# Attention decode over a cached GQA block: values as the streamed operand in four column groups, with the wanted tiles picked out by masks

## The chip, the cores and the metric

The kernel runs on one core of a Trainium2 chip. The metric is device time in microseconds (us) of one execution; the time of a version is the median of several executions. One more execution was recorded by the hardware profiler, and all lines of profile here come from it. PE is the matrix engine (TensorE), DVE the vector engine (VectorE), ACT the scalar engine (ScalarE), POOL GpSimd, and SP the engine that issues the DMAs.

## What is computed

Two layers, each an attention block with a cache and then a gated feed-forward block, with the same weights and the same cache in both. One new token for each of 4 sequences; 32 query heads share 8 key/value heads; 8192 cached positions of 128 numbers. Everything is bf16 at the inputs.

```python
def _A_ref(x, k_cache, v_cache, wq, wo):          # x: 4 x 1 x 512
    q = (x @ wq).reshape(B, Sq, 32, 128).transpose(0, 2, 1, 3)
    k = jnp.repeat(k_cache, 4, axis=1)            # cache: 4 x 8 x 8192 x 128
    v = jnp.repeat(v_cache, 4, axis=1)
    scores = jnp.einsum("bhqd,bhkd->bhqk", q, k) * (128 ** -0.5)
    p = softmax(scores, axis=-1)
    o = jnp.einsum("bhqk,bhkd->bhqd", p, v)
    return o.transpose(0, 2, 1, 3).reshape(B, Sq, 32 * 128) @ wo

def _B_ref(x, w_gate, w_up, w_down):
    return (silu(x @ w_gate) * (x @ w_up)) @ w_down

x = A_x
x = x + _A_ref(layernorm(x), ...)
x = x + _B_ref(layernorm(x), ...)
x = x + _A_ref(layernorm(x), ...)
x = x + _B_ref(layernorm(x), ...)
```

## The kernel before

**Units.** A unit is one key/value head `g` of one sequence `b`: 32 units a layer, 2 MB of keys and 2 MB of values each. SBUF has 8 slots of 2 MB (`kvf`); each load is one DMA from SP (`pump`, L307), issued as soon as a slot is free. Partition p of a slot holds positions 64p to 64p+63, so a slot is 64 tiles of 128 columns (one tile: one position from each partition). Three units of layer 0 stay in slots and are the first of layer 1. The feed-forward weights use two of the slots at the end of each layer; there the last seven loads are kept out of these two slots, and the very last V comes in four quarters (`split`, `NQ`).

**Keys.** DVE turns each eighth of a K slot in 32x32 blocks (`turn`, L392, eight 128x512 operations a unit). PE multiplies it with the queries (`scores`, L412, 4 matmuls of 256 columns an eighth). The scores of a unit are one 128x256 tile of PSUM: row 32a + 4q + h, column 32t' + i hold head h, and tile t = 8q + t' (q is the eighth, t' the tile within it).

**Softmax**, as five steps (`max_p`, `max_t`, `exps`, `turn_p`, `total`): row maximum on DVE (L418), turned on PE (L422), maximum per head on DVE (L425), spread by ACT (L428) and PE (L434), ACT for the bias (L437), the exponentials (L438) and their sums per head (L440), 32x32 transposes of the probabilities on DVE (L443), the total on PE (L446) and its reciprocal on DVE (L448).

**Values** (`values`, L482). For each tile t the 128x128 value tile is the stationary operand, and 32 columns of the turned probabilities stream past it, of which the first four are wanted; 64 matmuls accumulate into columns 0 to 31 of a PSUM bank (L493). The result is oT: output dimension on partitions, heads on columns. One DVE operation scales the four wanted columns (`scale_o`, L501). After the fourth unit of a head group `out_proj` multiplies with `wo` (L522, L525, L528, L513).

**What sets the order.** Each engine runs its instructions in the order in which the program issues them. Key and value work is a list of `blocks` with a cost in us each; `drain` runs them and after each lets `advance` take that cost off the first entry of `line`, the list of the small steps. A step is issued when its own gap has run down. `flush(u)` issues everything in `line` up to the steps of unit u before its values. When a unit's values are through, `scale_o` (and `out_proj` if it is due) go to the front of `line`. `turn` is issued when `keys` is called, about 2 us of blocks ahead of the scores. `_Sync` (L24 to L95) adds the semaphore waits.

**The ends of a layer.** After the last values come `out_proj`, `center`, the gate and up products (`ffn`, L599), the down products (L616), and in the last layer the transposes of the output (L665). The next layer's first key load goes into the slot that the gate and up weights used.

Of the kernel before, what the change touches and what calls it, by code (L numbers as in the profile page):

```python
# [103 lines left out]
def bass_interleave_layers__gqa_block_cached__swiglu_ffn__decode_kernel(  # L104
# [17 lines left out]
    REP = Hq // G  # L122
# [15 lines left out]
    NQ = 4  # L138
    NSLOT = 8
    NKEEP = 6  # L140
    WIDE = 32
# [4 lines left out]
    with ExitStack() as es:  # L146
# [32 lines left out]
        xx = sb("xx", [P, XB], FP32)  # L179
        lnv = sb("lnv", [P, B], FP32)  # L180
        rstd = sb("rstd", [P, B], FP32)
        xc = sb("xc", [P, XB], FP32)
        xn = sb("xn", [P, XB], BF16)
        oT = sb("oT", [P, Hq, B], BF16)
# [6 lines left out]
        pT = sb("pT", [P, 2, SW + WIDE], BF16)  # L191
        qT = pT[:, 1, 0:XQ].rearrange("p (b h) -> p b h", b=B)
        rl = sb("rl", [P, 2, REP], FP32)
        xoT = sb("xoT", [P, XB], BF16)
# [41 lines left out]
        for a in range(NA):  # L236
# [6 lines left out]
        T.op("dve", lambda e: e.memset(pT[:, :, SW:], 0.0), writes=["pT0", "pT1"])  # L243
        T.op("dve", lambda e: e.tensor_reduce(head[:], identf[:].rearrange("p (x h) -> p h x", h=REP), AX.X, ALU.max),
             reads=["ident"], writes=["head"])
        nc.scalar.preload_act_table_set("natural_log_exp_and_others")
# [195 lines left out]
        def turn_p(u):  # L442
            T.op("dve", lambda e: e.transpose(pT[:, turn_of[u], 0:SW], pb[:]), reads=["pb"], writes=[f"pT{turn_of[u]}"])  # L443
# [38 lines left out]
        def values(L, u):  # L482
            g, b = unit_gb(u)
            bk = OBK[turn_of[u]]

            def block(q):
                if q == 0:
                    flush(u)
                s = slot_of["V", L, u]

                for t in range(q * TB, (q + 1) * TB):
                    c0 = (t % TB) * QB + REP * q
                    T.op("pe", lambda e: e.matmul(bank(bk)[:, 0:WIDE], lhsT=kv[:, s, t * Dh:(t + 1) * Dh],  # L493
                                                  rhs=pT[:, turn_of[u], c0:c0 + WIDE], start=(t == 0), stop=(t == TT - 1)),
                         reads=[f"s{s}.{q}", f"pT{turn_of[u]}"], writes=[f"pb{bk}"], sig=(t % TB == TB - 1))
                if q == NB - 1:
                    finished(("V", L, u))
                    line[0:0] = rest

            def scale_o():  # L500
                T.op("dve", lambda e: e.tensor_tensor(oT[:, g * REP:(g + 1) * REP, b], bank(bk)[:, 0:REP],  # L501
                                                      rl[:, turn_of[u], :], ALU.mult),
                     reads=[f"pb{bk}", f"rl{turn_of[u]}"], writes=["oT"])

            rest = [[0.3, None, scale_o]]
            done.add((L, u))
            if all((L, g * B + k) in done for k in range(B)):
                rest.append([0.5, None, lambda: out_proj(g)])
            blocks.extend((0.2, lambda q=q: block(q)) for q in range(NB))
# [6 lines left out]
        def out_proj(g):  # L516

            pick = ident.rearrange("p (j e) -> p e j", e=REP)
            ob = bank(OUTB)[:, XB:2 * XB].rearrange("p (e b) -> p e b", b=B)
            for c in range(REP):  # L520
                for h in range(REP):
                    T.op("pe", lambda e: e.matmul(ob[h * QB:(h + 1) * QB, c, :], lhsT=pick[:, c, :],  # L522
                                                  rhs=oT[:, g * REP + h, :], start=True, stop=True),
                         reads=["oT", "ident"], writes=[f"pb{OUTB}"], sig=(h == REP - 1))
            T.op("dve", lambda e: e.tensor_copy(o4[:], ob), reads=[f"pb{OUTB}"], writes=["o4"])  # L525
            for nt in range(KT):
                for c in range(REP):
                    T.op("pe", lambda e: e.matmul(bank(OUTB)[:, nt * B:(nt + 1) * B],  # L528
                                                  lhsT=wo_sb[:, g, c, nt * P:(nt + 1) * P], rhs=o4[:, c, :],
                                                  start=(c == 0), stop=(c == REP - 1)),  # L530
                         reads=[f"wo{g // (G // 4)}", "o4"], writes=[f"pb{OUTB}"], sig=(c == REP - 1))
            add_to_x()
# [5 lines left out]
        def center():  # L538
# [8 lines left out]
            T.op("dve", lambda e: e.scalar_tensor_tensor(bk3(xc[:]), total, -1.0 / D, bk3(xT[:]),  # L547
                                                         op0=ALU.mult, op1=ALU.add),
                 reads=["x", f"pb{LNB}"], writes=["xc"])
            T.op("dve", lambda e: e.tensor_tensor(xx[:], xc[:], xc[:], ALU.mult), reads=["xc"], writes=["xx"])  # L550
            T.op("dve", lambda e: e.tensor_reduce(vs[:], xx[:].rearrange("p (k b) -> p b k", b=B), AX.X, ALU.add),
                 reads=["xx"], writes=["vs"])
# [34 lines left out]
        def ffn(last):  # L587
# [37 lines left out]
            if last:  # L625
                T.op("dve", lambda e: e.tensor_tensor(xoT[:], xT[:], bank(dn[-1])[:, 0:XB], ALU.add),
                     reads=["x", f"pb{dn[-1]}"], writes=["xoT"])
            else:
                add_to_x(dn[-1])
# [34 lines left out]
        for kt in range(KT):  # L664
            T.op("pe", lambda e: e.matmul(ob[0:B, kt * P:(kt + 1) * P], lhsT=xoT[:, kt * B:(kt + 1) * B],  # L665
                                          rhs=ident, is_transpose=True, start=True, stop=True),
                 reads=["xoT", "ident"], writes=[f"pb{LNB}"], sig=(kt == KT - 1))
# [32 lines left out]
```

## Time and profile before

| | |
|---|---|
| median of 3 runs | 665.35 us (664.87 to 666.32) |
| the profiled execution, its own time | 666.57 us |
| its span, first to last instruction | 664.7 us |
| PE, DVE, ACT busy | 502.1, 382.1, 89.9 us |
| HBM read | 273.88 MB, 412 GB/s over the span |
| mean granted PE clock | 0.82 |

A line of a group reads: line of the kernel, engine, operation, output<-input, shape, count | busy us in total, mean ns of one | idle us of the engine just before them, and what ended most of it. A line of the timeline reads: start us, duration us, engine, line, operation, count, and in brackets the idle time before it and what ended it. The DMA row gives the mean busy share of the 16 DMA engines in each of 40 slices, in tenths.

The chain that ended last, followed back from the last instruction, is made up of these shares of the span:

```profile
DMA 70%; PE 20%; DVE 4%; SPq 3%; issue 2%; POOL 0%; ACT 0%; DVEq 0%; POOLq 0%
```

### The profile page before, as it was taken

The page shows a single profiled execution, that of the slowest core. Times are in us where ns is not written, and L with a number is a line of the kernel's source. Part 1 is how long each engine was busy: PE and PEld are TensorE (multiplying, and loading weights), DVE is VectorE, ACT ScalarE, POOL GpSimd, SP SyncE. Part 2 cuts the span into 40 slices and gives each one's busy share as a digit, 9 for nine tenths or more (in the row PEclk, how much of TensorE's full clock was granted, in tenths as well). Part 3 has the DMA queues.
Part 4 walks back from the last instruction along what each step waited for, and adds up shares of the span by engine and source line. Part 5 has one row for each costly group of instructions (what it writes and reads, how often), then busy time and mean ns, then how long its engine had stood idle before and what let it go on. Part 6 is the DMA issues. An engine that isn't in the chain of part 4 may idle for free.

```text
span 664.7 us, 17302 instructions
## 1 busy us (share of the span) xinstructions
PE 502.1 (76%) x7656; PEld 400.1 (60%) x7656; DVE 382.1 (57%) x895; ACT 89.9 (14%) x331; POOL 19.9 (3%) x75
## 2 busy tenths in 40 slices
PE   1767687777768787876876999887787696786796
PEld 1545565655646565664664878765566565575575
DVE  1646475565566465575731289766566566566572
ACT  1010110110101110110110112110111110110120
POOL 0000000000000000000000000000000000000000
PEclk9887789877878778797785979986878977788885
DMA  9999999999999999999998899999999999999995
GB/s 366 424 423 418 430 431 423 425 425 429 427 424 425 427 426 425 426 428 424 424 404 344 331 426 430 425 424 427 426 427 424 428 426 426 426 425 429 425 414 210
DMA packets 23963, 275.00 MB, mean 414 GB/s; under 512 B 2376, under 2 KB 2384, under 8 KB 7888
## 3 DMA queue, kind: packets, MB, share of 16 engines
q1 hardware_dynamic: 23888, 273.89, 98.0%
q8 instruction: 60, 0.98, 0.6%
q14 instruction: 15, 0.12, 0.0%
HBM read 273.88 MB, written 0.00 MB: 412 GB/s over the span
## 4 chain that ended last, share of the span: by engine, by line
DMA 70%; PE 20%; DVE 4%; SPq 3%; issue 2%; POOL 0%; ACT 0%; DVEq 0%; POOLq 0%
DMA kvf<-in_A_k_cache_dram 68%; PE ps L412 13%; SPq L93 3%; DMA kvf<-in_B_w_down_dram 2%; DVE kvf L392 2%; PE ps L493 2%; PE ps L434 1%; PE ps L422 1%; DVE one L418 1%; PE ps L599 0%; PE ps L566 0%; PE ps L616 0%; DVE rl L448 0%; PE ps L446 0%; PE ps L541 0%
## 5 line engine op out<-in xcount | busy, mean ns | idle before, releaser
L392 DVE STREAM_TRANSPOSE kvf<-kvf 128x512 f32<-128x512 f32 x488 | 313.1, 677 | 193.5 <-DMA kvf<-in_A_k_cache_dram 193.5
L412 PE MATMUL ps<-kvf,zq 128*128 128x256 bf16 x2048 | 331.2, 318 | 9.5 <-DVE kvf L392 7.1
L412 PEld LDWEIGHTS ps<-kvf,zq 128*128 128x128 bf16 x2048 | 215.1, 113 | 69.4 <-DVE kvf L392 9.8
L493 PE MATMUL ps<-pT,kvf 128*128 128x32 bf16 x4096 | 123.0, 178 | 16.3 <-DVE rl L448 15.1
L493 PEld LDWEIGHTS ps<-pT,kvf 128*128 128x128 bf16 x4096 | 120.0, 97 | 23.9 <-issue 19.4
L422 PE MATMUL ps<-identf,one 128*1 128x128 f32 x64 | 19.2, 301 | 103.7 <-DVE one L418 103.7
L428 ACT ACTIVATE pb<-m 1x128 f32<-1x128 f32 x64 | 19.7, 308 | 391.9 <-DVE m L425 391.9
L422 PEld LDWEIGHTS ps<-identf,one 128*1 128x1 f32 x64 | 5.2, 81 | 107.7 <-DVE one L418 107.5
L403 POOL TENSOR_TENSOR zq<-scr,quad 128x64 bf16<-128x64 bf16 x64 | 18.8, 293 | 617.9 <-PE ps L412 550.5
L434 PEld LDWEIGHTS ps<-one,pb 1*128 1x128 f32 x128 | 24.4, 237 | 20.3 <-issue 18.1
L418 DVE TENSOR_REDUCE one<-ps 128x1 f32<-128x256 f32 x64 | 25.2, 394 | 10.6 <-PE ps L412 10.6
L443 DVE STREAM_TRANSPOSE pT<-pb 128x256 bf16<-128x256 bf16 x64 | 26.4, 412 | 8.3 <-ACT pb L438 7.7
L438 ACT ACTIVATE pb<-ps,one 128x256 bf16<-128x256 f32 x64 | 30.4, 474 | 2.1
L434 PE MATMUL ps<-one,pb 1*128 1x1 f32 x128 | 29.9, 300 | 0.5 <-ACT pb L428 0.5
L437 ACT ACTIVATE one<-ps 128x1 f32<-128x1 f32 x64 | 11.0, 171 | 137.2 <-PE ps L434 137.2
L446 PEld LDWEIGHTS ps<-rsm,one 128*128 128x128 f32 x128 | 20.8, 204 | 2.8 <-ACT rsm L440 0.6
L446 PE MATMUL ps<-rsm,one 128*128 128x4 f32 x128 | 19.8, 225 | 0.5 <-ACT rsm L440 0.5
L440 ACT ACTIVATE rsm<-head,one 128x4 f32<-128x4 f32 x64 | 19.0, 297 | 2.1
L425 DVE TENSOR_REDUCE m<-ps 1x4 f32<-1x128 f32 x64 | 15.9, 248 | 5.7 <-PE ps L422 5.0
L501 DVE TENSOR_TENSOR oT<-ps,rl 128x4 bf16<-128x4 f32 x64 | 7.9, 123 | 9.3 <-PE ps L493 8.9
L528 PE MATMUL ps<-o,wo_sb 128*128 128x4 bf16 x256 | 9.2, 167 | 4.9 <-DVE o L525 4.9
L513 DVE TENSOR_TENSOR xT<-xT,ps 128x16 f32<-128x16 f32 x21 | 3.6, 172 | 15.2 <-PE ps L528 11.1
(57 smaller groups left out, 108.3 us busy)
## 6 DMA issues: line engine op xcount, KB each, us to landing
kvf<-in_A_k_cache_dram SPq DMA_DIRECT2D x61, 2048.0 KB, 31.7
kvf<-in_A_v_cache_dram SPq DMA_DIRECT2D x58, 2048.0 KB, 32.3
wq_sb<-in_A_wq_dram SPq DMA_DIRECT2D x4, 1024.0 KB, 7.6
wo_sb<-in_A_wo_dram SPq DMA_DIRECT2D x4, 1024.0 KB, 35.2
kvf<-in_A_v_cache_dram SPq DMA_DIRECT2D x8, 512.0 KB, 19.7
kvf<-in_B_w_gate_dram SPq DMA_DIRECT2D x2, 1792.0 KB, 24.1
kvf<-in_B_w_down_dram SPq DMA_DIRECT2D x4, 768.0 KB, 16.3
kvf<-in_A_v_cache_dram SPq DMA_DIRECT2D x2, 1024.0 KB, 5.0
```

The source lines that it names most:

```text
L93: ins = self.eng[engname].dma_start(out_ap, in_ap)
L392: T.op("dve", lambda e: e.transpose(w, w), reads=[f"s{s}.{q}"], writes=[f"s{s}.{q}"])
L412: T.op("pe", lambda e: e.matmul(bank(bk)[:, 0:SW], lhsT=zq[:, c, z0:z0 + P], rhs=w[:, :, c // 2, :, c % 2], start=(q == 0 and c == 0), sto ...
L418: T.op("dve", lambda e: e.tensor_reduce(mx[:], bank(bk)[:, 0:SW], AX.X, ALU.max), reads=[f"pb{bk}"], writes=["mx"])
L422: T.op("pe", lambda e: e.matmul(bank(STEP)[0:1, 0:P], lhsT=mx[:], rhs=identf[:], is_transpose=True, start=True, stop=True), reads=["mx", " ...
L428: T.op("act", lambda e: e.activation(mrow.rearrange("p (x h) -> p x h", h=REP), m4[:].unsqueeze(1).to_broadcast([1, QB, REP]), ACTF.Copy), ...
L434: T.op("pe", lambda e: e.matmul(bank(STEP)[:, 0:1], lhsT=mrow, rhs=onesf[0:1, :], start=True, stop=True), reads=["pb", "onesf"], writes=[f ...
L438: T.op("act", lambda e: e.activation(pb[:], bank(bk)[:, 0:SW], ACTF.Exp, bias=nm[:], accum_out=rs[:]), reads=[f"pb{bk}", "nm"], writes=["p ...
L440: T.op("act", lambda e: e.activation(rsm[:], head[:], ACTF.Copy, scale=rs[:]), reads=["head", "rs"], writes=["rsm"])
L443: T.op("dve", lambda e: e.transpose(pT[:, turn_of[u], 0:SW], pb[:]), reads=["pb"], writes=[f"pT{turn_of[u]}"])
L446: T.op("pe", lambda e: e.matmul(bank(TOT)[:, 0:REP], lhsT=ones, rhs=rsm[:], start=True, stop=True), reads=["rsm", "onesf"], writes=[f"pb{T ...
L493: T.op("pe", lambda e: e.matmul(bank(bk)[:, 0:WIDE], lhsT=kv[:, s, t * Dh:(t + 1) * Dh], rhs=pT[:, turn_of[u], c0:c0 + WIDE], start=(t == ...
```

## The change

The operands of the value product swap places. Now 16 columns of the turned probabilities are the stationary operand and four value tiles (512 columns) stream past them. `NQ` becomes 2, `NV` = 4. A unit has two halves i; a half has 8 matmuls, one for each tile number t within the eighths; each streams tile t of the eighths 4i to 4i+3, and its 16 weight columns are those of the same four eighths, four heads each. Matmul t writes to the 16 partitions from 32 (t mod 4), so four column groups of the array are used in turn. A row of the result (eighth y, head h) holds four blocks of 128 columns, of which only block y is the row's own; the others are products with the wrong tile.

`own_tile` takes each row's own block: ACT copies block 0 scaled by mask column 0 into `acc` (128x128 fp32), and three DVE operations add blocks 1, 2, 3 times their masks (`own`, built at the start). `scale_o` then multiplies `acc` as weights with `head` (fp32, 4 columns) on PE, which adds the rows of one head over column groups and eighths and turns the result, and DVE scales it. `acc` is one buffer, shared by all units and, in its first columns, by `xc` and `xx` of `center`.

The last V of each layer comes in two halves. The two output banks are zeroed at the start, as the unwritten partitions of them are read. `oT` keeps two groups, and `xoT` is gone (`xn` serves). In `line`, the steps after a unit's values go behind earlier such steps but ahead of softmax steps that wait.

```diff
-    NQ = 4
+    NQ = 2
...
-    WIDE = 32
+    NV = NB // NQ
+    assert TB == 2 * NA and NV * REP <= QB
...
+        acc = sb("acc", [P, Dh], FP32)
+        own = sb("own", [P, NV], FP32)
+        xc, xx = acc[:, 0:XB], acc[:, XB:2 * XB]
...
+        T.op("dve", lambda e: e.memset(ps[:, OBK[0] * BANKF:(OBK[1] + 1) * BANKF], 0.0), writes=[f"pb{k}" for k in OBK])
...
+        T.op("dve", lambda e: e.tensor_reduce(acc[:, 0:QB], identf[:].rearrange("p (y h) -> p y h", h=REP), AX.X, ALU.max),
+             reads=["ident"], writes=["acc"])
+        T.op("dve", lambda e: e.tensor_reduce(own[:], acc[:, 0:QB].rearrange("p (a y) -> p y a", a=NA)[:, 0:NV, :],
+                                              AX.X, ALU.max),
+             reads=["acc"], writes=["own"])
...
-            def block(q):
-                if q == 0:
+            def block(i):
+
+                if i == 0:
                     flush(u)
                 s = slot_of["V", L, u]
-
-                for t in range(q * TB, (q + 1) * TB):
-                    c0 = (t % TB) * QB + REP * q
-                    T.op("pe", lambda e: e.matmul(bank(bk)[:, 0:WIDE], lhsT=kv[:, s, t * Dh:(t + 1) * Dh],
-                                                  rhs=pT[:, turn_of[u], c0:c0 + WIDE], start=(t == 0), stop=(t == TT - 1)),
-                         reads=[f"s{s}.{q}", f"pT{turn_of[u]}"], writes=[f"pb{bk}"], sig=(t % TB == TB - 1))
-                if q == NB - 1:
+                v = kv[:, s, :].rearrange("p (q t d) -> p t q d", t=TB, d=Dh)
+                for t in range(TB):
+                    j = t % NA
+                    c0 = t * QB + i * NV * REP
+                    T.op("pe", lambda e: e.matmul(bank(bk)[j * QB:j * QB + NV * REP, :],
+                                                  lhsT=pT[:, turn_of[u], c0:c0 + NV * REP], rhs=v[:, t, NV * i:NV * (i + 1), :],
+                                                  start=(i == 0 and t == j), stop=(i == NQ - 1 and t >= TB - NA)),
+                         reads=[f"s{s}.{NV * i + k}" for k in range(NV)] + [f"pT{turn_of[u]}"], writes=[f"pb{bk}"],
+                         sig=(t == TB - 1))
+                if i == NQ - 1:
                     finished(("V", L, u))
-                    line[0:0] = rest
+                    n = len([1 for x in line if x[1] is None])
+                    line[n:n] = rest
+
+            def own_tile():
+                T.op("act", lambda e: e.activation(acc[:], bank(bk)[:, 0:Dh], ACTF.Copy, scale=own[:, 0:1]),
+                     reads=[f"pb{bk}", "own"], writes=["acc"])
+                for k in range(1, NV):
+                    T.op("dve", lambda e: e.scalar_tensor_tensor(acc[:], bank(bk)[:, k * Dh:(k + 1) * Dh], own[:, k:k + 1],
+                                                                 acc[:], op0=ALU.mult, op1=ALU.add),
+                         reads=[f"pb{bk}", "own", "acc"], writes=["acc"])
 
             def scale_o():
-                T.op("dve", lambda e: e.tensor_tensor(oT[:, g * REP:(g + 1) * REP, b], bank(bk)[:, 0:REP],
-                                                      rl[:, turn_of[u], :], ALU.mult),
-                     reads=[f"pb{bk}", f"rl{turn_of[u]}"], writes=["oT"])
-
-            rest = [[0.3, None, scale_o]]
+                T.op("pe", lambda e: e.matmul(bank(LNB)[:, 0:REP], lhsT=acc[:], rhs=head[:], start=True, stop=True),
+                     reads=["acc", "head"], writes=[f"pb{LNB}"])
+                T.op("dve", lambda e: e.tensor_tensor(oT[:, g // (G - 1), :, b], bank(LNB)[:, 0:REP], rl[:, turn_of[u], :],
+                                                      ALU.mult),
+                     reads=[f"pb{LNB}", f"rl{turn_of[u]}"], writes=[f"oT{g // (G - 1)}"])
+
+            rest = [[0.1, None, own_tile], [1.0, None, scale_o]]
...
-            blocks.extend((0.2, lambda q=q: block(q)) for q in range(NB))
+            blocks.extend((0.8, lambda i=i: block(i)) for i in range(NQ))
```

## The prediction

> **What bounds the kernel now.** I read the page from the top (DMA rows, queues, chain), then windows of the layer ends, then the timeline there. First the page:
>
> ```profile
> DMA  9999999999999999999998899999999999999995
> q1 hardware_dynamic: 23888, 273.89, 98.0%
> q8 instruction: 60, 0.98, 0.6%
> L392 DVE STREAM_TRANSPOSE kvf<-kvf 128x512 f32<-128x512 f32 x488 | 313.1, 677 | 193.5 <-DMA kvf<-in_A_k_cache_dram 193.5
> L493 PE MATMUL ps<-pT,kvf 128*128 128x32 bf16 x4096 | 123.0, 178 | 16.3 <-DVE rl L448 15.1
> kvf<-in_A_v_cache_dram SPq DMA_DIRECT2D x58, 2048.0 KB, 32.3
> ```
>
> The reader is to see that the 16 DMA engines are full nearly throughout, that VectorE waits 193.5 us for keys, and that a load lands some 32 us after its issue: six loads of 5 us (2.1 MB at 426 GB/s) are queued. So inside a layer PE and DVE time is free as long as a unit (K and V, 9.85 us of DMA) takes them less. Only the layer ends are left. The timeline of the last one, in which I number a layer's units by their place, 0 to 31 (place 30's keys land at 630.45):
>
> ```profile
> 626.47 1.35 PE L493 MATMUL ps<-pT,kvf 128*128 128x32 bf16 x48
> 630.48 0.71 DVE L392 STREAM_TRANSPOSE kvf<-kvf 128x512 f32<-128x512 f32 x1 [4.66 <-DMA kvf<-in_A_k_cache_dram]
> 642.78 0.60 PE L412 MATMUL ps<-kvf,zq 128*128 128x256 bf16 x4
> 644.42 0.27 PE L422 MATMUL ps<-identf,one 128*1 128x128 f32 x1
> 649.73 1.85 PE L493 MATMUL ps<-pT,kvf 128*128 128x32 bf16 x64 [0.48 <-DVE rl L448]
> 651.61 0.17 DVE L501 TENSOR_TENSOR oT<-ps,rl 128x4 bf16<-128x4 f32 x1 [1.96 <-PE ps L493]
> ```
>
> From 630.48 the chain of waits follows PE and DVE, not data: all scores end at 643.38, values of place 31 at 651.58, their scaling at 651.78, the kernel at 664.7. The weights' DMA falls to 16 GB/s in the window 660 to 661, so it hides nothing that comes later than that. At the end of layer 0 it is the other way round:
>
> ```profile
> 347.45 0.91 PE L599 MATMUL ps<-xn,kvf 128*128 128x4 bf16 x28 [1.26 <-DMA kvf<-in_B_w_gate_dram]
> 351.94 1.63 PE L599 MATMUL ps<-xn,kvf 128*128 128x4 bf16 x56 [2.41 <-DMA kvf<-in_B_w_up_dram]
> 353.65 3.45 SPq L93 DMA_DIRECT2D kvf<-in_A_k_cache_dram  x2
> 355.72 1.02 PE L616 MATMUL ps<-scr,kvf 128*128 128x4 bf16 x32 [1.04 <-DMA kvf<-in_B_w_down_dram]
> ```
>
> There each weight is waited for, and the next key load goes out when the up product frees its slot (353.65).
>
> **The products.** Removed per unit: 64 matmuls, 1.85 us. Added: 16 of 512 columns, four column groups. No such shape is in the trace. Score matmuls give the rate: x12 takes 1.50 and x8 1.05 us at granted clock 1.00, so 0.113 us per 256 columns (0.21 at clock 0.50: 2.72 for 12, 1.89 for 8). One after another 16 x 512 would be 3.6 us. The nearest row in column groups:
>
> ```profile
> 383.18 0.39 PE L580 MATMUL ps<-pT,identf 128*32 128x112 bf16 x16 [0.37 <-DVE pT L571]
> ```
>
> These 1792 columns would take 0.79 us in series; 0.39, of which 0.21 is the last one's own duration, says that four run at once. So 16 x 512 / 4 = 0.9 us plus a 0.15 tail: 1.05 us at full clock, 1.85 at half; bounds 0.9 and 3.6 (7 at half clock).
> [...]
>
> **The evacuation.** Before: one DVE scaling of 128x4 (0.12 to 0.17 us). After, per unit: one ACT copy of 128x128 (between L437, 1 column, 0.171, and L438, 256 columns, 0.474: 0.32); three DVE operations of 128 columns (L571: 16 columns 0.175, 112 columns 0.274, so 0.29; each waits for the one before, +0.03 as from L608 to L609 to L610: 0.96 in all); an fp32 matmul of 4 columns in two passes like L446 (0.36; 0.6 at half clock, as L541); the scaling. With 0.04 per hop that is 1.95 us where 0.2 stood. DVE gains 0.9 us a unit on 6.0 (382.1/64), under 9.85.
>
> **Order of the instructions, end of layer 1.** This decides. In the changed kernel's DVE order, place 28's turned probabilities (L443) stand behind place 30's first key transpose, and its three new operations between the second and third. Before, 48 of 64 value matmuls of place 28 ran at 626.47, ahead of that landing. After, from the landing: transpose 0.67 + L443 0.40 = 1.1; values to 2.2 (3.05 at half clock); ACT 0.37 and three DVE 0.96 to 3.5 (4.4), with DVE idle for 1.3 of it. Then in order 14 transposes at 0.64, scaling 0.12, two L425 0.25, L443 0.45, L448 0.1, L418 0.36: 10.5, and the last score matmuls 0.9: scores end 14.85 (15.75) after the landing. Before: 643.38 - 630.45 = 12.9. Cost 1.9 to 2.8, I take 2.3.
>
> Next, PE. Before, the softmax steps of place 31 (L422, L434) ran between values of 29 and 30. After, PE's order is values 29 and 30, both evacuations, out_proj, and only then L422. From the end of scores: total 0.3; values 0.95, 0.95; the evacuation of 29 ends 3.1 (0.3 + 1.05 + 0.35 + 1.0 + 0.4); 30's copy needs the one buffer acc, which 29's fp32 matmul reads, so it starts there: +1.8 and scaling 0.2, 5.1; L522 0.5, L525 0.2, L528 0.63: 6.4; L422 to the value matmuls 2.95 (0.31 + 0.31 + 0.34 + 0.43 + 0.21 + 0.6 + 0.35 + 0.4, by L422, L425, L428, L434, L437, L438, L440, L446): 9.35; values 1.05 (1.85), evacuation 1.95 (2.25): 12.35 (13.45). Before: 651.78 - 643.38 = 8.4. Cost 3.95 to 5.05; I take 4.6, as the clock is 0.50 from 650 on and PE idles more.
> Behind it lie 12.9 us as before, with one 0.98 stall (652.18, "issue") that may go or stay: 0 to -1, taken as 0. Layer-1 end: +6.9.
>
> **End of layer 0.** The same chain without the middle out_proj (1.33) ends at 323.2 + 14.85 + 12.35 - 1.33 = 349.1 at full clock, 1.1 later with the half-clock second part; I take 349.4, as the clock there was 1.00 until 342. Before it was 343.8, with a wait for V's last quarter. The gate wait (1.26), up wait (2.41) and down wait (1.04) take most: gate from 352.0 (2.6 us after the scaling, as before), done 354.1, up done 355.8 against 353.57, down done 358.0 against 356.7. The next key load goes out 2.2 us late; the loads after it follow the PE, 1.2 late; faster values there give back 0.4. Cost 1.0 (0 to 2.5). The last V in halves spares SP two issues of 0.33 us ahead of the weights and makes the first product wait for twice as much; the later chain covers that wait, and SP runs loads ahead. If the weights' cover were gone, all 5.6 would be paid.
>
> **Instruction fetch.** Of 17302 instructions 6144 go (3072 matmuls and their loads) and some 520 come; q8 moves 0.98 MB in 0.6% of the span, 4.0 us. A third less: -1.3 by time, -0.8 by bytes, 0 if it hides: -0.9.
>
> **The rest at nothing:** the start-up memset of two banks and two small reductions on DVE (about 2 us by L418's and L244's rates) fall into DVE's wait for x; if that cover were gone, 2 us. Smaller buffers move no transfer. Each V slot is held until the next-but-one K lands, one of six queued loads; if the queue were that short it would cost 5 us a unit.
>
> Sum: 6.9 + 1.0 - 0.9 = +7.0. Against the profiled execution (span 664.7, 666.57 with what lies around it) 673.6; the runs' median is 1.2 lower, so 672.4.
>
> **Rivals.**
> *A, faster:* the layer-1 end is set by the weights after all, and the evacuations hide. Place: L616 at 660.08. For it: the DMA runs until 660.5. Against: L616 waited for DVE, not DMA, so slack is about 0.5 us and the chain grows by 7. Under 0.5 of growth it decides; then instruction fetch (-1.3) and earlier slots at layer 1's start (DMA share 0.63 and 0.66 in 372 to 376, up to -0.7) leave 663.4. 7%.
> *B, the new work hides inside the order* (the 4.6 and 2.3 shrink under 1 each because DVE runs ahead): about 666, 5%. Against: the semaphore waits of the new order.
> *C, units become chain-bound:* landing to the next K's first transpose is 7.6 us by the sum above (8.6 at half clock, some 1 more where out_proj falls) against 9.85. If it came to 10.35, 0.5 x 60 units = +30: 702. 5%.
> *D, column groups in series:* values 3.6, +2.55 a unit; the chain 10.15 against 9.85, 0.3 x 55 = 16, and four exposed products 10: 698. 3%. [...]
>
> **Numbers.** Forecast 80%: 672.4, own range 668 to 677.5 (low: 1.9 + 3.95 + 0 - 1.3 - 1 = +3.5, 668.9; high: 2.8 + 5.05 + 2.5 - 0 and a code stall of 1: +11, 676.7). For 8 in 10, 667 to 678, as C and D lie far off. What a measurement can tell from no change is 0.2%, 1.3 us: faster 0.07, same 0.05, slower 0.88.
>
> **What would show it.** Values of 16 matmuls at 1.0 to 1.9 us; the 128x128 DVE operation near 0.29; scores ending 15 us after place 30's keys land, and 13 us from there to the last scaling; DMA share still 1.0 inside the layers; q8 near 0.65 MB. Wrong if the last scaling comes less than 25 us after that landing (A, B), or if DVE no longer waits for keys in the layers (C, D).

## The result, and the profile after

The changed kernel takes 672.39 us (median of 7 runs, 668.56 to 673.63) against 665.49 (664.87 to 666.61) on the same chip: 1.0082 times as long, 95% interval 1.0067 to 1.0098. The forecast was 672.4. The single runs fall into two groups, 668.6 to 669.8 and 672.4 to 673.6, which the kernel before does not do; the profiled execution (669.12, span 667.2) belongs to the lower group, 2.5 above the span before, while four of the seven runs, and with them the median, belong to the upper. Why there are two groups is one of the things the experiments had to find out.

The page of the changed kernel: DMA share by slices, the queue of the instruction fetch, and two of the costliest groups (busy us, mean ns of one | idle before it, releaser).

```profile
DMA  9999999999999999999997999999999999999992
q8 instruction: 37, 0.61, 0.4%
L399 DVE STREAM_TRANSPOSE kvf<-kvf 128x512 f32<-128x512 f32 x488 | 316.7, 684 | 64.5 <-DMA kvf<-in_A_k_cache_dram 64.4
L516 DVE SCALAR_TENSOR_TENSOR acc<-ps,own,acc 128x128 f32<-128x128 f32 x192 | 67.3, 350 | 52.2 <-ACT acc L513 44.0
```

The DMA engines are as full as before (mean share 1.01 over 8 to 340 us in both profiles). Instruction fetch (q8) fell from 0.98 to 0.61 MB. VectorE waits 64.4 us for keys instead of 193.5: the units use much of the free time that they had, but not all of it. So the difference should lie where no free time was, at the layer ends. The timeline of the last one (start, duration, idle before it; keys of place 30 land at 627.18):

```profile
627.18 0.71 DVE L399 STREAM_TRANSPOSE kvf<-kvf 128x512 f32<-128x512 f32 x1 [1.71 <-DMA kvf<-in_A_k_cache_dram]
628.36 1.04 PE L502 MATMUL ps<-kvf,pT 128*16 128x512 bf16 x16 [1.17 <-DVE rl L455]
629.92 1.12 DVE L516 SCALAR_TENSOR_TENSOR acc<-ps,own,acc 128x128 f32<-128x128 f32 x3 [0.71 <-ACT acc L513]
639.26 1.28 DVE L399 STREAM_TRANSPOSE kvf<-kvf 128x512 f32<-128x512 f32 x2
640.04 1.50 PE L419 MATMUL ps<-kvf,zq 128*128 128x256 bf16 x12
641.61 1.90 PE L502 MATMUL ps<-kvf,pT 128*16 128x512 bf16 x32
648.13 0.37 PE L429 MATMUL ps<-identf,one 128*1 128x128 f32 x1
651.50 1.88 PE L502 MATMUL ps<-kvf,pT 128*16 128x512 bf16 x16
655.72 0.17 DVE L523 TENSOR_TENSOR oT<-ps,rl 128x4 bf16<-128x4 f32 x1 [0.68 <-PE ps L521]
```

The order is the one read out of the diff: one evacuation (629.92) inside the last transposes, the values of 29 and 30 together (641.61), both their evacuations (until 646.94), the projection, and only then L429 (648.13; L422 in the kernel before), which opens the softmax of place 31. Set beside the kernel before:

| stretch (us) | before | after | difference |
|---|---|---|---|
| start to landing of place 30's keys, layer 1 | 630.45 | 627.18 | -3.3 |
| landing to end of all scores | 12.93 | 14.36 | +1.4 |
| end of scores to last scaling done | 8.40 | 14.35 | +5.95 |
| last scaling to end of span | 12.9 | 11.3 | -1.6 |
| span | 664.7 | 667.2 | +2.5 |

The 1.6 include the 0.98 us stall of the kernel before, which is gone, and some 0.4 of a second one there (an "issue" wait ahead of the last up products, 659.37).

### The profile page after: what moved, and what is told of

It reads as the page before. It is cut to its first block, busy times and chain, and to the rows that moved or that the text cites. A ratio compares the mean times of both kernels' runs of the same rounds, so it can differ in the third digit from the quotient of the medians.

```text
span 667.2 us, 11563 instructions
## 1 busy us (share of the span) xinstructions
PE 494.5 (74%) x4712; PEld 308.7 (46%) x4712; DVE 452.5 (68%) x1089; ACT 113.3 (17%) x395; POOL 19.8 (3%) x75
## 4 chain that ended last, share of the span: by engine, by line
DMA 51%; PE 22%; DVE 20%; ACT 4%; issue 2%; SPq 1%; POOL 0%; DVEq 0%; POOLq 0%
DMA kvf<-in_A_k_cache_dram 51%; DVE kvf L399 12%; PE ps L419 9%; PE ps L502 6%; DVE acc L516 5%; PE ps L441 2%; ACT acc L513 2%; PE ps L550 1%; ACT pb L445 1%; PE ps L453 1%; ACT pb L435 1%; DVE pT L450 1%; SPq L93 1%; DVE m L432 0%; PE ps L621 0%
## 5 line engine op out<-in xcount | busy, mean ns | idle before, releaser
L399 DVE STREAM_TRANSPOSE kvf<-kvf 128x512 f32<-128x512 f32 x488 | 316.7, 684 | 64.5 <-DMA kvf<-in_A_k_cache_dram 64.4
L419 PE MATMUL ps<-kvf,zq 128*128 128x256 bf16 x2048 | 317.8, 296 | 21.8 <-DVE kvf L399 16.8
L419 PEld LDWEIGHTS ps<-kvf,zq 128*128 128x128 bf16 x2048 | 186.4, 104 | 123.1 <-DVE kvf L399 44.7
L502 PE MATMUL ps<-kvf,pT 128*16 128x512 bf16 x1024 | 77.9, 432 | 43.1 <-DVE rl L455 42.7
L516 DVE SCALAR_TENSOR_TENSOR acc<-ps,own,acc 128x128 f32<-128x128 f32 x192 | 67.3, 350 | 52.2 <-ACT acc L513 44.0
L521 PE MATMUL ps<-head,acc 128*128 128x4 f32 x128 | 27.2, 283 | 38.5 <-DVE acc L516 38.1
L502 PEld LDWEIGHTS ps<-kvf,pT 128*16 128x16 bf16 x1024 | 22.3, 93 | 65.0 <-issue 52.1
L513 ACT ACTIVATE acc<-ps,own 128x128 f32<-128x128 f32 x64 | 23.5, 367 | 154.0 <-PE ps L502 150.6
L521 PEld LDWEIGHTS ps<-head,acc 128*128 128x128 f32 x128 | 21.6, 212 | 58.8 <-DVE acc L516 58.7
L450 DVE STREAM_TRANSPOSE pT<-pb 128x256 bf16<-128x256 bf16 x64 | 26.9, 421 | 25.8 <-ACT pb L445 25.7
L453 PE MATMUL ps<-rsm,one 128*128 128x4 f32 x128 | 24.1, 259 | 15.2 <-ACT rsm L447 15.2
L453 PEld LDWEIGHTS ps<-rsm,one 128*128 128x128 f32 x128 | 20.0, 197 | 29.2 <-ACT rsm L447 28.7
L429 PE MATMUL ps<-identf,one 128*1 128x128 f32 x64 | 19.2, 299 | 0.0
L455 DVE RECIPROCAL rl<-ps 128x4 f32<-128x4 f32 x64 | 10.6, 166 | 12.4 <-PE ps L453 12.3
```

The lines of the kernel that those rows point to most:

```text
L399: T.op("dve", lambda e: e.transpose(w, w), reads=[f"s{s}.{q}"], writes=[f"s{s}.{q}"])
L419: T.op("pe", lambda e: e.matmul(bank(bk)[:, 0:SW], lhsT=zq[:, c, z0:z0 + P], rhs=w[:, :, c // 2, :, c % 2], start=(q == 0 and c == 0), sto ...
L450: T.op("dve", lambda e: e.transpose(pT[:, turn_of[u], :], pb[:]), reads=["pb"], writes=[f"pT{turn_of[u]}"])
L453: T.op("pe", lambda e: e.matmul(bank(TOT)[:, 0:REP], lhsT=ones, rhs=rsm[:], start=True, stop=True), reads=["rsm", "onesf"], writes=[f"pb{T ...
L502: T.op("pe", lambda e: e.matmul(bank(bk)[j * QB:j * QB + NV * REP, :], lhsT=pT[:, turn_of[u], c0:c0 + NV * REP], rhs=v[:, t, NV * i:NV * ( ...
L513: T.op("act", lambda e: e.activation(acc[:], bank(bk)[:, 0:Dh], ACTF.Copy, scale=own[:, 0:1]), reads=[f"pb{bk}", "own"], writes=["acc"])
```

## The experiments

All times are medians; the kernel before ran beside them at 665.26 to 665.36. Diffs are against the changed kernel unless said otherwise.

**The changed kernel once more**, to catch the upper group of runs.

> The changed kernel unchanged, to see its scatter: its seven times fall into 668.6 to 669.8 and 672.4 to 673.6. My theory: the order at the layer ends makes it slower by about 7 us behind the landing of place 30's keys in every execution, and what differs between executions is when these keys land (627.2 in the profile so far). Rival: the layer-end chain itself takes 3 to 4 us longer in the slow ones. By the theory a profile of a slow execution shows the chain from landing to the last scaling at 28.7 +- 0.5 again and a later landing; by the rival the landing at 627 and a chain of 32.

672.16 us (670.5 to 672.88), ratio 1.0093 (1.0078 to 1.0107), and the profile, of span 670.4, is of the upper group. Two of the five runs, 670.5 and 670.92, lie in the gap, so the groups are not as sharp as the first seven runs had them. At the end of layer 1 the theory holds: place 30's first transpose starts at 629.93 instead of 627.18 (it is the second of the two in this line, and the first of a unit takes 0.71), and the last scaling ends 29.1 later, against 28.7.

```profile
629.20 1.44 DVE L399 STREAM_TRANSPOSE kvf<-kvf 128x512 f32<-128x512 f32 x2
```

Summed from the start, the bytes moved are the same to 0.1 us in both profiles until 340 us; by 380 the upper one is 3.4 us behind, and it stays 3.4 to 3.5 behind to the end. So the two profiles part at the end of layer 0. Windows of the two there (length, then PE, PEld, DVE, ACT, POOL busy, granted clock, DMA share, GB/s), the lower group's first:

```profile
318.00:320.00 2.00, 1.94 (x18) 1.44 (x16) 1.49 (x4) 0.31 (x1) 0.00 (x0) 1.00 1.02 434
322.00:324.00 2.00, 1.79 (x24) 0.87 (x16) 1.62 (x5) 0.37 (x1) 0.00 (x0) 1.00 0.98 410
```

And the same windows of the upper group's:

```profile
318.00:320.00 2.00, 2.00 (x11) 1.32 (x10) 1.45 (x4) 0.00 (x0) 0.00 (x0) 0.50 1.06 451
322.00:324.00 2.00, 1.78 (x11) 0.97 (x14) 0.62 (x3) 1.03 (x4) 0.29 (x1) 0.50 0.94 401
```

The upper run has a stretch of half clock just there. Its timeline, values of place 28 to the issue of layer 1's next key load:

```profile
320.50 0.71 DVE L399 STREAM_TRANSPOSE kvf<-kvf 128x512 f32<-128x512 f32 x1 [0.39 <-DMA kvf<-in_A_k_cache_dram]
323.72 1.88 PE L502 MATMUL ps<-kvf,pT 128*16 128x512 bf16 x16
337.81 1.90 PE L502 MATMUL ps<-kvf,pT 128*16 128x512 bf16 x32
356.62 2.37 SPq L93 DMA_DIRECT2D kvf<-in_A_k_cache_dram  x2
```

The keys of place 30 land at the same time (320.50 against 320.58). The softmax of 28 then runs at half clock, its values start at 323.72 instead of 321.76, those of 29 start 2.8 late (337.81 against 335.01), and the next key load goes out 2.4 late, at 356.62 instead of 354.25.

**The steps at the layer ends in another order.** The softmax steps of place 31 go between the value products of 29 and 30; the matmul that ends each evacuation goes behind the products of the next unit. (a, b, c are places 29, 30, 31; of a unit's steps `ra`, `rb`, `rc` the first is `own_tile`, the second `scale_o`, and a third `out_proj` where it is due.)

```diff
-            drain(0.0)
-            flush()
+            end_of_layer(L)
...
+            va(0), va(1)
+            max_t_()
+            ra[0]()
+            vb(0), vb(1)
+            exps_()
+            ra[1]()
...
+            turn_p_()
+            rb[0]()
+            total_()
+            vc(0), vc(1)
+            for fn in rb[1:]:
+                fn()
+            for fn in rc:
+                fn()
```

> The changed kernel with another order at the layer ends alone: the softmax steps of place 31 run between the values of places 29 and 30, place 31's values come straight after its total, and the second evacuation and out_proj behind them. Theory (PE's order at the layer end costs 5 us): from the end of scores to the last scaling 9 to 9.5 us where the changed kernel has 14.3, the time 5 +- 1 us under the changed kernel's, about 667. Rival (the weights' landing sets the end): not more than 1 us under it. Rival (the loss is spread over the units): no change.

663.13 us (662.58 to 664.91), ratio 0.9966 (0.9953 to 0.998): 9 us under the changed kernel, and faster than both. Timeline of its last layer end:

```profile
626.17 0.71 DVE L399 STREAM_TRANSPOSE kvf<-kvf 128x512 f32<-128x512 f32 x1 [1.35 <-DMA kvf<-in_A_k_cache_dram]
640.59 1.04 PE L502 MATMUL ps<-kvf,pT 128*16 128x512 bf16 x16
641.56 0.27 PE L429 MATMUL ps<-identf,one 128*1 128x128 f32 x1
645.03 0.61 PE L502 MATMUL ps<-kvf,pT 128*16 128x512 bf16 x8 [0.35 <-DVE pT L450]
650.26 0.17 DVE L523 TENSOR_TENSOR oT<-ps,rl 128x4 bf16<-128x4 f32 x1 [0.68 <-PE ps L521]
```

From the landing to the values of 29 it takes 14.42 us, as in the changed kernel (14.43); from there to the last scaling 9.84 instead of 14.28. L429 now runs 1 us after the values of 29 start, and the values of 31 begin 4.4 us after those of 29 instead of 9.9. The chain of evacuations was not shortened by a single instruction; it only no longer stands ahead of a softmax that could have run beside it. These 4.4 us (14.28 to 9.84) are half of the 9; the next two runs look for the others.

**The same order at one layer end only** (`end_of_layer` where `L == 1`, or where `L == 0`).

> The order that tail_order used at both layer ends (softmax steps of place 31 issued between the value products of 29 and 30, the evacuations after them) now at the end of layer 1 alone. Theory: both layer ends cost, each its part. In tail_order the stretch from the end of the scores to the last scaling of layer 1 was 9.9 us against 14.35 in the changed kernel, and what lies behind it was the same 11.3, so this kernel gains 4.4: about 667.8 against 672.2, and its single runs still fall into two groups some 3.4 apart, as those of the changed kernel do, because layer 0's end is left as it is. Rival: the end of layer 0 is hidden by the waits for the gate, up and down weights, and all 9.0 us that tail_order gained come from layer 1's end: 663, one group of runs. Second rival: nearly all came from layer 0's end and the start of layer 1, and layer 1's end is set by the landings of the weights: 671 to 672.

> The same order at the end of layer 0 alone. Theory: 9.0 - 4.4 = 4.6 gained, about 667.6, of which part is the slower group of runs that goes (the later the chain of layer 0's end, the later the next key load goes out; with the shorter chain the gate, up and down waits cover it again), so the spread is under 2.5. Scores of place 31 to the last scaling of layer 0 in 9 instead of 12.9 us, next key load out 2 to 4 us earlier. Rival (layer 0 hidden): 672, as the changed kernel, in the same two groups.

Layer 1 alone: 666.79 us (665.83 to 668.59, 10 runs), against 672.16 a gain of 5.4. Layer 0 alone: 668.26 (667.34 to 668.56), a gain of 3.9. Together 9.3, against 9.0 for both at once: the two ends add up, and neither rival holds. The layer-1 runs still spread over 2.8 us, the five of layer 0 over 1.2; but the two groups that were expected of the layer-1 runs are not there. And the 3.9 count from an upper-group time: against the lower group (668.6 to 669.8) layer 0's new order is worth about 1, so most of its gain is that the late executions are gone. For the end of layer 0, the profiles that differ in the order alone, side by side (clock as means of 2 us windows):

| profile | granted clock, 316 to 326 | values of 28 | next key load |
|---|---|---|---|
| before | 0.50 until 322 | | 353.65 |
| changed, lower group | 1.00 | 321.76 | 354.25 |
| tail_l1 (layer 0 as changed) | 0.50 to 0.91 until 322 | 322.85 | 355.44 |
| changed, upper group | 0.50 from 318 on | 323.72 | 356.62 |
| tail_order | 1.00 | 321.75 | 352.08 |
| tail_b (below) | 0.50 to 0.86 until 322 | 322.95 | 352.06 |
| tail_l0 | 0.50 to 0.84, 318 to 324 | 323.37 | 352.03 |

In the changed kernel's order the next key load follows the granted clock; in tail_order's it goes out at the same time whatever the clock was, although the values of 28 start up to 1.6 us apart. There the chain has slack again: in tail_order the second half of place 31's values waits for its load, and the down product for its weights.

```profile
341.29 1.03 PE L502 MATMUL ps<-kvf,pT 128*16 128x512 bf16 x8 [1.06 <-DMA kvf<-in_A_v_cache_dram]
352.08 3.43 SPq L93 DMA_DIRECT2D kvf<-in_A_k_cache_dram  x2
354.13 1.02 PE L673 MATMUL ps<-scr,kvf 128*128 128x4 bf16 x32 [1.02 <-DMA kvf<-in_B_w_down_dram]
```

**The evacuation issued later.**

```diff
-            rest = [[0.1, None, own_tile], [1.0, None, scale_o]]
+            rest = [[0.9, None, own_tile], [1.0, None, scale_o]]
```

> The changed kernel with the evacuation (ACT copy and the three 128x128 DVE operations) issued 0.8 us of planned work later behind its value products, so that one or two key transposes stand ahead of it on DVE. Theory: the 1.5 us that the scores of the last units ended later than before come from DVE standing still before these operations (0.71 us of idle at full clock in the profile of the changed kernel, 1.2 at half clock): scores end 13.6 instead of 14.36 after place 30's keys land, and the time falls by 0.7 to 2, to 670.2 to 671.5. Rival: the later scaling and the later release of the one buffer acc cost as much at the layer ends, where nothing else is left to run in between: 672 to 673.5.

672.67 us (671.51 to 673.51), ratio 1.0108 (1.0093 to 1.0122): no gain, in the rival's range. Timeline of its last layer end:

```profile
628.86 0.71 DVE L399 STREAM_TRANSPOSE kvf<-kvf 128x512 f32<-128x512 f32 x1 [0.28 <-DMA kvf<-in_A_k_cache_dram]
630.20 0.45 DVE L450 STREAM_TRANSPOSE pT<-pb 128x256 bf16<-128x256 bf16 x1 [0.62 <-ACT pb L445]
633.19 1.08 DVE L516 SCALAR_TENSOR_TENSOR acc<-ps,own,acc 128x128 f32<-128x128 f32 x3
643.67 0.61 PE L502 MATMUL ps<-kvf,pT 128*16 128x512 bf16 x8
```

The transposes do run on ahead of L516, which no longer waits. But the values of 29 start 14.81 us after the landing, against 14.43 in the changed kernel. The wait was not taken out, it moved to the front: the clock was 0.50 from 621.8 to 625.3, before the landing, the softmax of 28 was late, and DVE waited 0.62 for its probabilities (630.20) and 0.33 for its total (630.97), 0.95 where the changed kernel's profile has 0.71 ahead of L516. So the time shows no gain, but this profile does not show whether an evacuation without a wait would have gained; that stays open.

**Two of the three DVE operations left out** (their tiles are missing from the result).

```diff
-                for k in range(1, NV):
+                for k in range(1, 2):
```

> The changed kernel with one instead of three 128x128 DVE operations in the evacuation (the third and fourth masked tile of each half are left out of the output). 0.75 us less of DVE per unit. Theory: the scores of layer 1 end later than before because of these operations themselves (DVE has one of three sets, 1.12 us, between place 30's landing and the end of the scores, beside 0.7 of idle), so scores end 0.7 earlier (13.6 after the landing), and from there to the last scaling the three evacuations in a row, two of them on the path for each, take 2 x 0.75 or 3 x 0.75 less (14.35 to 12.1 to 12.9); layer 1's end gains 2.2 to 3.0 and layer 0's with it 1 to 3: 666.5 to 669. Rival: the scores' end is set by PE and the softmax steps, and the acc buffer's wait by the products: under 1.5 us of gain in all, 671 or more.

664.91 us (664.15 to 665.59), ratio 0.999 (0.9982 to 0.9999): 7.3 us gained, where 3.2 to 5.7 were expected. The timeline of the last layer end:

```profile
625.20 0.71 DVE L399 STREAM_TRANSPOSE kvf<-kvf 128x512 f32<-128x512 f32 x1 [1.55 <-DMA kvf<-in_A_k_cache_dram]
627.94 0.35 DVE L516 SCALAR_TENSOR_TENSOR acc<-ps,own,acc 128x128 f32<-128x128 f32 x1 [0.71 <-ACT acc L513]
638.86 2.22 PE L502 MATMUL ps<-kvf,pT 128*16 128x512 bf16 x32
650.85 0.17 DVE L523 TENSOR_TENSOR oT<-ps,rl 128x4 bf16<-128x4 f32 x1 [0.68 <-PE ps L521]
```

Landing to values: 13.66 instead of 14.43, 0.77 less, which is what the two operations took (1.12 - 0.35) in the one set that runs there. Values to last scaling: 12.16 instead of 14.28, 2.1 less for three sets. So at this end the DVE operations are paid almost one for one, 2.9 of the 3.1 that four sets had less. The remaining 4.4 lie ahead of the landing: place 30's keys land at 625.20, 2.0 earlier than in the lower group's profile and 4.7 earlier than in the upper's. The next key load of layer 0 went out at 351.88, as early as with tail_l0, so the loads set the time there again. What was too small in the expectation is that step.

**Place 31's evacuation ahead of place 30's projection**, on top of tail_order.

```diff
-            for fn in rb[1:]:
-                fn()
-            for fn in rc:
-                fn()
+            rb[1]()
+            rc[0]()
+            for fn in rb[2:] + rc[1:]:
+                fn()
```

> tail_order with one more change of order: at both layer ends the evacuation of place 31 is issued ahead of the output projection that place 30's group waits for, not behind it. In tail_order the first of place 31's three DVE operations began at 648.46, 1.26 us after its ACT copy was done (647.20), behind the projection's cast and add. Theory: these 1.2 us lie on the path: 661.9 against 663.1. Rival: the landing of the last values or the projection itself sets the end, and the time is that of tail_order, 663.1; or the projection ahead of it comes later by as much.

663.37 us (662.02 to 663.48): as tail_order; the rival holds. Counted from the landing of place 30's keys (626.62, against 626.17 in tail_order), place 31's three DVE operations do start 1.3 earlier (at 647.62 against 648.46), but the matmul that reads their sum was still issued behind the projection, so it waits on PE instead. The last scaling ends 23.49 after the landing, against 24.26 in tail_order: in these two profiles a gain of under 1 us, which the times (662.02 to 663.48 and 662.58 to 664.91) do not show.

**The products in one column group and in two.**

```diff
-                    j = t % NA
-                    c0 = t * QB + i * NV * REP
+                    j = 0
+                    c0 = t * QB + i * NV * REP
...
-                                                  start=(i == 0 and t == j), stop=(i == NQ - 1 and t >= TB - NA)),
+                                                  start=(i == 0 and t == 0), stop=(i == NQ - 1 and t == TB - 1)),
```

For two groups it is `j = t % 2`, the start condition stays, and the stop is `t >= TB - 2`. (`own` is cleared for the rows of the groups not used.)

> The changed kernel with all 16 products of a unit written by column group 0 (masks of the other partitions zeroed). Theory (four groups run at once in the changed kernel, 1.04 us a unit at full clock): one group takes 3.6 to 3.9 us a unit at full clock and 7 at half; the units' chain grows to about 10.2 us against 9.85 of DMA, the layer ends by 3 x 2.6, so 685 to 700 us. Rival (groups never ran at once): values and time as in the changed kernel.

> The changed kernel with the 16 products in two column groups instead of four (one_column_group had one; there the 16 took 3.62 us at full clock against 1.04 in four). Theory: the time of the products goes with the number of groups that run at once, so 16 take 1.81 + 0.1 = 1.9 us at full clock; the unit's chain, 7.6 to 8.2 us, becomes 8.5 to 9.1 and stays under the 9.85 of its DMA, so that, other than with one group, only the layer ends and the start of layer 1 pay: two exposed products of 0.87 at each end and a slower catching up, 676 to 680. Rival: the weight loads set the pace of any number of groups below four, or the half-clock stretches make the units chain-bound: above 690. Second rival: the products were hidden at the ends too: 672.

One group: 779.72 us (776.26 to 782.41), ratio 1.1711 (1.168 to 1.1741). Two: 681.94 (679.6 to 683.05), 1.0244 (1.0225 to 1.0263). Timeline of the one-group kernel, a unit's products and their weight loads at full clock:

```profile
210.44 3.62 PE L504 MATMUL ps<-kvf,pT 128*16 128x512 bf16 x16
210.44 3.12 PEld L504 LDWEIGHTS ps<-kvf,pT 128*16 128x16 bf16 x16
```

Timeline of the two-group kernel, a unit's products:

```profile
635.59 1.90 PE L504 MATMUL ps<-kvf,pT 128*16 128x512 bf16 x16
```

3.62, 1.90 and, in four groups, 1.04 us: the groups run at once, as the transposing matmuls of the kernel before had let one expect. The starts of the products in successive units give the length of a unit's chain where it does not wait for data: 8.17 us in the changed kernel, 9.71 for the unit with a projection, so (3 x 8.17 + 9.71) / 4 = 8.56 on average. Two groups: 9.02 and 10.55, 9.40. One group: 10.74 and 12.27, 11.12. Only the last is over the 9.85 that DMA takes for a unit, by 1.27 in each of some 57 units, or 72 of the 107 us (the rest was not divided). The expectation, 685 to 700, missed by 80: it had put the chain at 10.2, little over DMA's. Two groups stay under 9.85, and pay at the boundary (the next key load at 358.21, 4.0 later than in the changed kernel), by never catching up with the data in layer 1, and in the last values (3.58 at half clock); the 1.9 us are as forecast, the total is 2 above its range.

**Extra instructions, to price their fetch**: 48 tiny products behind the values of 52 of the 64 units, results unused, once on the changed kernel and once on tail_order.

```diff
+                pos = unit_order[L].index(u)
+                if i == NQ - 1 and 4 * L <= pos < NU - 4:
+                    for k in range(48):
+                        T.op("pe", lambda e: e.matmul(bank(OUTB)[0:REP, 2 * XB:2 * XB + B], lhsT=pT[:, turn_of[u], 0:REP],
+                                                      rhs=ident[:, 0:B], start=True, stop=True),
+                             reads=[f"pT{turn_of[u]}", "ident"], writes=[f"pb{OUTB}"], sig=(k == 47))
```

> The changed kernel with 48 tiny matmuls of 4 columns added to each unit's values, outside the first four places of layer 1 and the last four of both layers: 52 units, 4992 instructions more, nothing read of them. PE has time for them inside a layer. Theory (instruction fetch shares the full DMA engines): place 30's keys land 0.8 to 3 us later than in the changed kernel and the time is that much longer; instruction bytes rise from 0.61 to about 0.93 MB. Rival (fetch hides): landing and time as the changed kernel's within 0.5.

> tail_order with the 48 tiny products per unit of dummy_products (their results are used by nothing). In dummy_products the extra instructions came together with a later end of layer 0, so that 5.2 us could not be divided. With the order of tail_order the next key load went out at 352.03 to 352.08 in three profiles, whatever clock was granted before, so that here only the fetch of the instructions should be left. Theory: some 20 more fetch packets at 0.05 to 0.07 us of DMA progress each (23 fewer gave 1.7 us between the kernel before and the changed one): 663.1 + 1.0 to 1.4, so 664.1 to 664.5, the same bytes reached 1.0 to 1.4 us later than in tail_order. Rival: fetches are hidden, and the 5.2 us were the PE time of the tiny products at the layer ends alone: 663.1, no difference in the bytes.

On the changed kernel 677.35 us (675.79 to 679.77), ratio 1.0177 (1.0155 to 1.0198), 5.2 more where at most 3 were expected. Its bytes fall 0.55 us behind by 340, and its next key load goes out at 359.32, 5.1 after the lower group's and 2.7 after the upper's, so that fetch and the boundary can't be told apart there. On tail_order 667.61 (667.09 to 667.88), 1.0031 (1.002 to 1.0041). That is 4.5 over tail_order, where 1.0 to 1.4 were expected. Its page shows the fetch queue:

```profile
q8 instruction: 57, 0.93, 0.6%
```

And its timeline the 48 products of one unit:

```profile
612.04 1.34 PE L510 MATMUL ps<-identf,pT 128*4 128x4 bf16 x48
```

20 more fetch packets, but also 1.34 us of PE in a unit. By bytes, this run falls behind tail_order by 0.47 us up to 340 and by another 0.45 from 388 to 628, stretches in which the DMA engines are full (mean share 1.01 in both) and no load is issued late; between them, 1.4 are lost at the layer boundary, where the next key load goes out at 355.30 instead of 352.08. So fetch is not hidden: about 0.9 us for 20 packets, as far as the tiny products did not slow the loads in some other way; the greater part of the 4.5 is not fetch, and the run does not divide it further. The expectation was wrong in taking the tiny products' own time as covered.

**The last values in halves, in the kernel before** (`NQ = 4` to `NQ = 2` there).

> The kernel before, with only the last values of a layer loaded in halves instead of quarters. Theory: nothing, 665.3 within 0.7: the values of place 31 wait for the softmax steps, not for their load, and SP runs ahead. Rival: the first products of place 31 now wait for twice as much data at the end of layer 0, 0.5 to 1.3 us: 665.8 to 666.6; or two issues of 0.33 us fewer ahead of the weights: 664.6.

665.4 us (664.46 to 666.94), ratio 1.0 (0.9989 to 1.001): nothing, as the prediction had it.

## Why the prediction came out right, and where its parts did not

The time was met to the microsecond, and that is luck. Set against the profile before, the forecast was +7.0; the profiles of the changed kernel show +5.7 (upper group) and +2.5 (lower). With one run more in the lower group the median would have been near 670, still within the range. And the errors of the terms cancel: in the upper group's profile the landing of place 30's keys comes 0.5 earlier than before (forecast 0.1 later), from there to the last scaling it takes 7.8 more (forecast 6.9), and behind it 1.6 less (forecast 0).

- *The bound and the place.* Right. Inside the layers the units stay under their DMA time (8.56 against 9.85), and both ends pay; with their order mended the change is a gain.
- *The products.* 1.05 us at full clock and 1.85 at half forecast, 1.04 and 1.88 measured. Even in one group the 16 products with their full-height loads take 3.62 us, 0.226 for 512 columns, which is the score matmuls' rate of 0.113 for 256. The loads hide there too: their 3.12 us lie inside those 3.62.
- *The evacuation.* 0.29 us forecast for a DVE operation, 0.350 measured; 0.32 for the ACT copy, 0.367. The DVE price was drawn out from a 16 and a 112 column row of another operation (L571), the ACT price taken between two rows of operations with other outputs (L437, L438); both were too cheap.
- *Landing to scores.* +2.3 forecast (1.9 to 2.8), +1.43 measured, at full clock. The step that failed is the DVE work behind the evacuation: the sum gave it 10.5 us, 14 transposes at 0.64 and the small operations at their own durations. Measured it is 9.5, from the end of L516 (631.04) to the end of the last transposes (640.54), as an operation starts before the record of the one ahead of it has ended: four transposes take the 2.40 from 634.19 to the start of L450 at 636.59, 0.60 each. The evacuation itself ended 3.86 after the landing, not 3.5. The idle of DVE was 0.71 there, not 1.3. drop_two shows that the DVE work is paid in full here (0.77 for 0.77); what a wait costs own_late leaves open.
- *Scores to last scaling.* +4.6 forecast (3.95 to 5.05), +5.95 measured. Mechanism and order were right, as tail_order and tail_l1 show; the sum was short in every evacuation (each DVE set 1.12, not 0.96) and in the half clock, which covers everything from L429 on and makes the softmax 3.4 instead of 2.95 and the last evacuation 2.5 instead of 2.25.
- *Behind the last scaling.* Taken as 0, with 0 to -1; -1.6 measured.
- *Layer 0.* +1.0 forecast (0 to 2.5), on the argument that the waits for gate, up and down take most. The step that failed is this one: in the changed kernel no product there waits for gate or up any more, and the cover is used up. The next key load is 0.6 late in the lower group and 3.0 in the upper. By bytes, from 340 to 388, the boundary gains 0.5 against the kernel before in the lower group's profile and loses 2.9 in the upper's, on both sides outside the range; tail_l0 had 3.9 us of the median back there.
- *Instruction fetch.* -0.9 forecast (0 to -1.3). The bytes are 0.76 us ahead of the kernel before at 340, and gain about 0.5 more between 388 and 644, so -1.3, if all of it is fetch; at tail_dummy's price (0.9 for 20 packets) the 23 packets fewer would be an estimated -1.0. Between the two, about 0.5 is gained in the lower group; layer 1's start loses less DMA time there (share 0.92 in 372 to 376 against 0.65).
- *Not forecast:* in the lower group's profile the landing of place 30's keys is 3.3 earlier, the bytes about 1.7. The keys of successive units land 9.8 us apart, but in the kernel before every ninth lands 1.2 to 1.5 later than that (134.1, 223.7, 313.2 and 451.2, 540.7, 630.5), and place 30 of layer 1 is one of these; in the changed kernel it is not (617.4, 627.2), and the late landings that its trace shows are fewer (192.5, 271.7, 568.5). Why those landings are late was not settled.
- *The spread.* Not forecast at all. The prediction had both clocks in its chain, as bounds. That the granted clock at one place differs from run to run, and that the new order passes this on to the next key load, is what after_again and tail_l1 (between the two in both) show; it rests on three profiles.
- *The rivals.* A (weights set layer 1's end) and B (new work hides) fall with the 14.35 us. C and D (chain-bound units) fall with the 64.4 us that DVE still waits; two groups are near that point and one is past it. D's price was far too low: one_column_group, which is D built, took 780, not 698, as a unit's chain came to 11.12 and not 10.15.

## What to carry to other kernels

When a cheap last step is replaced by a chain over three engines, look at what stands behind it in each engine's order where the streaming ends: here the same instructions in another order turned +7 us into -2. Price such a chain at every place where no load hides it, and at both clocks; where it uses up the last slack, the run-to-run differences of the clock become differences of the time (here the next key load went out at 354.25 or at 356.62). When summing a busy engine's work, take the distance from one start to the next in the trace and not the durations, which overlap (here 0.60 us from one key transpose to the next, with records of 0.66 to 0.71). And before moving work to fill a wait, see in the profile that the wait went away: in own_late it had only moved.

## What the runs showed of the hardware that was not expected

The same instructions at the same place were granted full clock from 318 to 326 us in one execution (1.00, the lower group's profile) and half clock in another (0.50, the upper group's). In the lower group's profile the granted clock changes 43 times, in that of the kernel before 75 times, and within each of the two all these times lie whole multiples of 3.41 us apart, to 0.02: 288.7 and 339.9, say, in the lower group's (15 x 3.41). The upper group's 282.7, 316.8, 327.1 and 344.1 (10, 3 and 5 x 3.41) fit the same step, and are no multiple of it away from the lower group's: the times fall otherwise from execution to execution. Where they fall does not settle the clock by itself: tail_l0 and tail_order, the same program up to the end of layer 0, have them at the same offset from the start (319.2 and 322.6 in the one, 339.7, or 5 x 3.41 later, in the other), and yet over 319.2 to 322.6 the one was at half clock and the other at full. Nor does the busy share of PE tell the clock of a span: 81% went with 0.958 in one_column_group, 82% with 0.859 in tail_dummy, whose many products are tiny.
